# Attention with a score threshold, then a top-1 mixture of experts: tables, gathers, weights, loads and logits around the seam placed elsewhere, and fp16 weights of three double tiles made by VectorE

## The chip, the cores and the metric

One core of a Trainium2 chip runs the whole program in one launch. The metric is the device time of that program in microseconds (us); lower is better. Engines are named as in the profile: PE (TensorE matmuls), PEld (its weight loads), DVE (VectorE), ACT (ScalarE), POOL (GpSimd), SP (SyncE, which here only issues DMAs).

## The reference

Shapes: q, k, v are 8 x 8 x 576 x 64 (batch, heads, tokens, head size), tau is 0.02; w_gate is 512 x 8, w1 is 8 x 512 x 1024, w2 is 8 x 1024 x 512. All are float32.

```python
scores = scale * q @ k^T
thresh = max(scores, axis=-1) - tau
scores = where(scores >= thresh, scores, -1e9)
attn = exp(scores - max); attn = attn / (sum(attn) + 1e-9)
x = (attn @ v), heads side by side        # 4608 tokens x 512
logits = x @ w_gate
expert_idx = argmax(logits); gate_w = its softmax probability
for e in range(8):
    xe = x[expert_idx == e]
    out[expert_idx == e] = gate_w * (max(xe @ w1[e], 0) @ w2[e])
```

## The kernel before, in words

**Attention.** The 64 heads are worked as 32 pairs, the 8 batches as four pairs each. A pair takes 11 steps (st_order, s_order): each step makes one 128 x 512 tile of scores of a later pair (s_unit, whose row minima of the negated scores go to nm, L368) and one transposed tile of this pair (st_unit, st, L404 and L405). fp32 is kept by splitting numbers into fp16 high and low parts, so a product is three fp16 matmuls, or two wider ones through the stacked tiles QK, CQ and ck. On each transposed tile ACT makes the exponential e (L421), DVE sets what is below the threshold to zero (mask, L424), and for each double tile of 1024 columns ACT casts to the fp16 weights ph (L429) and POOL makes the remainder pl (L430), one of them on DVE for the last pair (PLV). av_piece (L474) multiplies ph and pl with the values.

**The row maxima** of a pair are turned by PE (turn in parts, pst, L379), the threshold is added and split in three fp16 rows by a chain over ACT and DVE (L384 to L387), and SP puts these rows into CQ (L392). The next pair's transposed tiles wait for them.

**After each batch** (finish): ACT and DVE make the reciprocals of the sums, one(j) makes a 128-token tile of x (xn, L528), high splits it into the row buffer R (L535 cast, L536 rest), SP turns it with a DMA transpose (xTg, L543), logits multiplies it with the gate (lg, L561), route finds the expert of each token on DVE (L591 to L602), ranks counts the places by matmuls (rk, L610 to L613), and POOL scatters the rows R into the DRAM buffer xs, sorted by expert (L633). For the last batch b = 7 the logits are spread over steps (LS) and route's chain is put into the plan at once.

**The expert part** runs slots of 128 tokens: tables0, tables1 and tables2 (after the routes of batches 5, 6 and 7) compute on DVE which rows of xs a slot reads (counts with pc, L663; table_first, L683 to L692; row, L658). fetch(m) gathers a slot on POOL (Rm, spare or R <- xs, L850) and SP turns it (xTm, L860); gemm1 makes h (L914, relu on ACT L902 and DVE L903), gemm2 makes y (L947), ACT scales it (L958) and POOL scatters it to the output (L961). Slots 0 to 2 use tiles of their own, slots 3 and 4 the tile "spare", later slots the five parts of R, which are free only once the rows of batch 7 were scattered. The order of the halves is written in `turns`: first gemm1 of slots 0, 1, 2, then gemm2 of 0 and 1, gemm1 of 3, gemm2 of 2, and so on.

**Expert weights.** An expert has eight chunks of 128 x 1024 fp32 (w1: four, w2: four): load_w issues the DMA (wf, L794), split_w casts the high half on ACT (wb, L809) and makes the low half on DVE (L817). For expert 0 the low half goes over PE: the high half is multiplied with the identity into PSUM (hi_w, L254), and DVE subtracts it (L255).

**What sets the order.** A plan: plan(k, f) puts work at step k, after(d, f) d steps on. hurry gives work a higher priority. A step is one round of the main loop; in it due() runs the planned work at three places (FRONT, MID, END). The expert part is a generator, experts(), of chunks of about 12 matmuls; RATE(k) says how many chunks are issued in a step: 0 before KM = KEND - km, rate/100 from there to KEND = 352 (the end of the last pair's steps), 1 after. moe(c, ...) puts work at chunk c. Numbers of the plan are in TUNE. The five engines then run their own queues in the order so written (moved a little by the scheduler where program order isn't kept), and wait for each other by semaphores. SP's queue is in order: a DMA whose data isn't there yet holds all DMAs behind it.

The touched places: TUNE, the tiles cks and cqs, parts.turn, st_unit.mask and cast, ranks (its last lines), load_w, tables0 to tables2, and the plan of the split_w and load_w of expert 0. The line numbers here and in the rows are those of the kernel before; in the changed kernel they are 3 lines more at L392, 11 more at L430, L536 and L591, and 18 more from L794 on.

## Time and profile before

| | us |
|---|---|
| median of three runs | 1001.75 (998.88 to 1005.34) |
| the profiled execution, its own time | 997.49 |
| its span in the trace | 995.8 |
| PE busy | 941.6 (95%) |
| DVE busy | 700.4 (70%) |
| ACT busy | 654.1 (66%) |
| POOL busy | 563.1 (57%) |

The mean granted clock of PE over the span was 0.983. All times in the rows below are those of one profiled execution, counted from the start of its span; the 1.7 us between the span and that execution's own time lie around it. The attention's pairs run from about 20 to 575 us, the seam between the two parts lies between about 520 and 660 us, and the expert part fills the rest.

### The profile page before, as it was taken

What the parts mean: (1) busy time and instruction counts of PE and PEld (TensorE: products, weight loads), DVE (VectorE), ACT (ScalarE), POOL (GpSimd) and SP (SyncE); (2) the same over time, 40 slices, a digit from 0 to 9 for tenths busy, and PEclk for the clock granted to TensorE, in tenths of its full rate; (3) what the DMA queues carried; (4) which work ended last, traced back from release to release, by engine and by line L of the source; (5) the groups of instructions that cost most, each with busy time, mean ns of one, the idle gap of its engine ahead of it and who ended that gap; (6) DMA issues with size and microseconds to landing.
All of it is one profiled execution on the core that took longest, in us unless ns stands there. A gap on an engine that the chain in (4) does not pass through costs nothing. (4 is left out here: it accounts for less than half of the span.)

```text
span 995.8 us, 28654 instructions
## 1 busy us (share of the span) xinstructions
PE 941.6 (95%) x11548; PEld 606.9 (61%) x11548; DVE 700.4 (70%) x1413; ACT 654.1 (66%) x1114; POOL 563.1 (57%) x470
## 2 busy tenths in 40 slices
PE   7899999999999999999998998799999999999997
PEld 2355556556566555565664675677666776667684
DVE  7899999989999889999999664816342333423560
ACT  2689897988989888989989853534243332433651
POOL 6366886895986977969969851343122121221121
PEclk8899999999999999999999899999999999999999
DMA  7553454464555646546636569998664756556630
GB/s 199 146 137 75 140 141 134 121 170 113 148 153 137 160 96 175 146 113 161 150 91 193 88 171 276 379 188 247 170 218 116 224 151 180 164 156 214 217 109 27
DMA packets 142750, 159.20 MB, mean 160 GB/s; under 512 B 96403, under 2 KB 112789, under 8 KB 142614
## 3 DMA queue, kind: packets, MB, share of 16 engines
q1 hardware_dynamic: 126598, 100.33, 39.9%
q0 software_dynamic: 9248, 29.45, 9.1%
q10 hardware_dynamic: 6768, 27.55, 8.8%
q8 instruction: 92, 1.51, 0.6%
q14 instruction: 44, 0.36, 0.1%
HBM read 90.24 MB, written 19.44 MB: 110 GB/s over the span
## 5 line engine op out<-in xcount | busy, mean ns | idle before, releaser
L430 POOL TENSOR_TENSOR pl<-e,ph 128x1024 f16<-128x1024 f32 x158 | 335.8, 2133 | 102.3 <-ACT ph L429 64.0
L421 ACT ACTIVATE e<-st,ntau 128x512 f32<-128x512 f32 (+1 forms) x352 | 222.7, 649 | 53.0 <-PE st L405 49.2
L424 DVE SCALAR_TENSOR_TENSOR e<-st,e 128x512 f32<-128x512 f32 (+1 forms) x352 | 220.3, 636 | 11.2 <-ACT e L421 10.5
L947 PE MATMUL y<-wb,hl 128*128 128x512 f16 (+1 forms) x1056 | 202.9, 361 | 0.0
L368 DVE TENSOR_REDUCE nm<-s 128x1 f32<-128x512 f32 x300 | 188.4, 633 | 20.4 <-PE s L358 18.4
L914 PEld LDWEIGHTS <-wb 128*128 128x128 f16 x2304 | 189.4, 98 | 19.8 <-issue 1.5
L914 PE MATMUL h<-xTm,wb 128*128 128x256 f16 (+2 forms) x2112 | 194.7, 253 | 1.0 <-DMA xTm<-Rm 1.0
L474 PE MATMUL av<-vop,ph 128*128 128x65 f16 (+3 forms) x3072 | 187.9, 195 | 2.3 <-ACT x L484 2.0
L474 PEld LDWEIGHTS <-ph 128*128 128x128 f16 (+1 forms) x3072 | 158.8, 100 | 46.4 <-issue 21.7
L474 PE MATMUL av<-vop,pl 128*128 128x65 f16 (+1 forms) x1536 | 167.8, 194 | 5.4 <-POOL pl L430 5.2
L429 ACT CAST ph<-e 128x1024 f16<-128x1024 f32 x160 | 166.3, 1039 | 6.1 <-DVE e L424 5.7
L474 PEld LDWEIGHTS <-pl 128*128 128x128 f16 (+1 forms) x1536 | 137.1, 100 | 37.0 <-issue 11.2
L947 PEld LDWEIGHTS <-hl 128*128 128x128 f16 (+1 forms) x1056 | 94.2, 100 | 98.6 <-issue 3.0
L817 DVE SCALAR_TENSOR_TENSOR wb<-wf,wb 128x1024 f16<-128x1024 f32 x88 | 103.9, 1221 | 56.3 <-ACT wb L809 54.8
L404 PE MATMUL st<-QK 128*128 128x512 f16 (+3 forms) x640 | 139.3, 296 | 1.5 <-DVE lo L255 0.8
L405 PE MATMUL st<-CQ,ck 128*128 128x512 f16 (+3 forms) x640 | 137.8, 290 | 0.5 <-DMA CQ<-ptT 0.5
L356 PE MATMUL s<-QK 128*128 128x512 f16 (+1 forms) x600 | 129.1, 292 | 2.9 <-DMA QK<-hi 2.1
L358 PE MATMUL s<-ck,CQ 128*128 128x512 f16 (+1 forms) x600 | 127.6, 288 | 1.5 <-DMA CQ<-hi 1.5
L961 POOL DMA_INDIRECT out_dram<-o,gt x40 | 47.8, 1194 | 138.6 <-ACT o L958 128.1
L809 ACT ACTIVATE wb<-wf 128x1024 f16<-128x1024 f32 x96 | 98.0, 1050 | 35.5 <-DMA wf<-in_w_dram 18.6
L902 ACT ACTIVATE hl<-h 128x512 f16<-128x512 f32 (+1 forms) x80 | 45.8, 572 | 109.9 <-PE h L914 108.3
L865 DVE COPY gt<-R 128x1 f32<-128x1 f32 x33 | 5.0, 153 | 129.7 <-DMA out_dram<-o,gt 112.5
(195 smaller groups left out, 1018.4 us busy)
## 6 DMA issues: line engine op xcount, KB each, us to landing
wf<-in_w_dram SPq DMA_DIRECT2D x96, 512.0 KB
qkf<-in_qk_dram ACTq DMA_DIRECT2D x30, 576.0 KB
vf<-in_v_dram ACTq DMA_DIRECT2D x15, 640.0 KB
QK<-hi SPq DMA_DIRECT2D x64, 144.0 KB
QK<-lo SPq DMA_DIRECT2D x64, 72.0 KB
QK<-hi SPq DMA_DIRECT2D x64, 72.0 KB
ck<-lo SPq DMA_DIRECT2D x64, 72.0 KB
CQ<-hi SPq DMA_DIRECT2D x64, 64.0 KB
```

The lines of the kernel that those rows point to most:

```text
L356: nc.tensor.matmul(sc[rows, oc], d["QA"][a][:, cols], d["KB"][a][:, CH[c]], start=True, stop=False)
L358: nc.tensor.matmul(sc[rows, oc], d["CQ"][:, at:at + cols.stop - cols.start], d["CK"][a][:, CH[c]], start=False, stop=True,)
L368: nc.vector.tensor_reduce(o, sc[:, 0:width(t)], axis=AX.X, op=ALU.max, negate=True)
L404: nc.tensor.matmul(sc[rows, oc], d["KB"][a][:, cols], d["QA"][a][:, CH[c]], start=True, stop=False)
L405: nc.tensor.matmul(sc[rows, oc], d["CK"][a][:, cols], d["CQ"][:, q], start=False, stop=True)
L421: nc.scalar.activation(pf, sc, AF.Exp, bias=ntau, scale=0.125 / SS)
L424: nc.vector.scalar_tensor_tensor(pf, sc, 0.0, pf, ALU.is_ge, ALU.mult)
L429: nc.scalar.copy(h, pd)
L430: (nc.vector if (n, t) in PLV else nc.gpsimd).tensor_tensor(l, pd, h, ALU.subtract)
L474: nc.tensor.matmul(av[:, 0:D] if z == 2 else av, l if z == 1 else h, vop[:, tv, W:W + D] if z == 2 else vop[:, tv, 0:W], start=i in (0, NT ...
L914: nc.tensor.matmul(o, Wt[:, c, wh, f], x, start=c == 0 and z == 0, stop=c == 3 and z == 2,)
L947: nc.tensor.matmul(o, h[:, hh], Wt[:, f, wh, c], start=f == 0 and z == 0, stop=f == 7 and z == 2)
```

## The change

- **Weights made by DVE.** For the last pair's tiles 2, 3, 8, REST, 6 and 7 (three double tiles) the fp16 weights ph come from a second DVE instruction, h = (sc >= 0) * pf with fp16 output, for each of the six tiles; the ACT cast of these three double tiles is gone. POOL's (or DVE's) remainder pl stays.
- **Expert 0's late chunks.** The tiles ck and CQ are allocated in twos, and the fp32 chunks w2[2] and w2[3] of expert 0 are loaded into the halves that are dead by then, at steps 2 and 3 of pair 30, by SP; before they went through the two wf buffers at KEND + 1 and KEND + 3. The last four splits of expert 0 stand at KEND + 1, 3, 5, 7; before at KEND + 1, 3, 9, 12.
- **Expert 1's loads** are issued by ACT's queue; before by SP's. They are 4 steps apart (w1d; before 5), and their splits are planned from chunk 26 on, 4 apart (w1a, w1b; before chunk 22, 5 apart).
- **Expert part's start.** km 12 (16) and rate 40 (15): four chunks are issued before KEND; before two.
- **Logits and ranks of the last batch.** lg7 is 22 (14): the logits stand 8 steps later. The ranks follow 6 steps after the route's start; before at once.
- **Tables.** tables0 and tables1 run 5 steps after the ranks; before after all scatters of their batch. Their fetches stay at the old place (lag). tables0 is hurried no longer.
- **Threshold of the last two pairs.** The transpose pst takes a bank of the scores' pool; for the last pair its chain is planned at once and hurried.

```diff
-lg7=14, km=16, rate=15, w1d=5, w1a=-42, w1b=5
+lg7=22, km=12, rate=40, w1d=4, w1a=-38, w1b=4
...
-    cks = [[cpool.tile([P, S], F16, name=f"ck_{i}_{a}") for a in range(2)] for i in range(NQ)]
-    cqs = [op.tile([P, 9 * P], F16, tag=f"CQ{i}", name=f"CQ_{i}", bufs=1) for i in range(NQ)]
+    ck2 = [cpool.tile([P, 2, 2, S], F16, name=f"ck_{i}") for i in range(NQ // 2)]
+    cq2 = [op.tile([P, 2, 9 * P], F16, tag=f"CQ{i}", name=f"CQ_{i}", bufs=1) for i in range(NQ // 2)]
+    cks = [[ck2[i // 2][:, i % 2, a] for a in range(2)] for i in range(NQ)]
+    cqs = [cq2[i // 2][:, i % 2] for i in range(NQ)]
...
-            ps = ps_m.tile([P, 512], F32, tag="m", name=f"pst_{n}")
+            pool, tag = (ps_sc, "sc") if n >= NPAIR - 2 else (ps_m, "m")
+            ps = pool.tile([P, 512], F32, tag=tag, name=f"pst_{n}")
...
-            chain(1, [
+            chain(int(n < NPAIR - 1), [
...
-            ])
+            ], n == NPAIR - 1)
...
-        (after if n >= 1 else lambda k, f: hurry(f)())(1, turn)
+        if n == 0:
+            hurry(turn)()
+        else:
+            after(1, hurry(turn) if n == NPAIR - 1 else turn)
...
+        direct = n == NPAIR - 1 and t in DIRECT
+
         def mask():
+            if direct:
+                nc.vector.scalar_tensor_tensor(h[:, j], sc, 0.0, pf, ALU.is_ge, ALU.mult)
...
-            nc.scalar.copy(h, pd)
+            if not direct:
+                nc.scalar.copy(h, pd)
...
-                after(wait + dist * n, TABLES[b])
+                at = 5 if b < B - 1 else wait
+                after(at, lambda: TABLES[b](wait + dist * n - at))
-        after(0 if b == B - 1 else RK[b], ranks)
+        after(6 if b == B - 1 else RK[b], ranks)
...
+        if (e, w) == (0, 1) and c >= 2:
+            wf = (ck2, cq2)[c - 2][0]
...
+            nc.sync.dma_start(wf, w12[e, :, c, w])
+            return
-            load = nc.sync.dma_start(wf, w12[e, :, c, w])
+            load = (nc.scalar if e == 1 else nc.sync).dma_start(wf, w12[e, :, c, w])
...
+    DIRECT = (2, 3, 8, REST, 6, 7)
...
-        t = k + WS0 + WSD * i if i < 4 else KEND + (1, 3, 9, 12)[i - 4]
+        t = k + WS0 + WSD * i if i < 4 else KEND + 1 + 2 * (i - 4)
         plan(t, lambda i=i: split_w(*wseq[i]))
-        if i + 2 < 8:
+        if i < 4:
             plan(t, lambda i=i: load_w(*wseq[i + 2]))
-    TABLES = {B - 3: hurry(tables0), B - 2: tables1, B - 1: tables2}
+        elif i >= 6:
+            plan(NSTEP * (NPAIR - 2) + i - 4, lambda i=i: load_w(*wseq[i]))
+    TABLES = {B - 3: tables0, B - 2: tables1, B - 1: tables2}
```

POOL's queue before, at the end of the attention: R is the low half of a row tile of batch 6, pl a double tile's remainder, Rm the gathers of slots 0 and 1.

```order
L536 TENSOR_TENSOR R<-xn_3_12175,R 128x4x128
L430 TENSOR_TENSOR pl_6_12201<-e_6_12199,ph_6_12200 128x1024
L430 TENSOR_TENSOR pl_0_12318<-e_0_12316,ph_0_12317 128x1024
L850 DMA Rm_12214<-xs,row_12173 128x514
L850 DMA Rm_12258<-xs,row_12173 128x514
L430 TENSOR_TENSOR pl_2_12351<-e_2_12349,ph_2_12350 128x1024
```

The same place of POOL's queue in the changed kernel (its L868 is L850 of before, L441 is L430):

```order
L547 TENSOR_TENSOR R<-xn_3_12167,R 128x4x128
L868 DMA Rm_12202<-xs,row_11771 128x514
L868 DMA Rm_12248<-xs,row_11771 128x514
L441 TENSOR_TENSOR pl_6_12193<-e_6_12191,ph_6_12192 128x1024
L441 TENSOR_TENSOR pl_0_12310<-e_0_12308,ph_0_12309 128x1024
L441 TENSOR_TENSOR pl_2_12350<-e_2_12348,ph_2_12349 128x1024
```

The two gathers moved ahead of two remainders.

SP's queue before, at the last batch: xTg are the transposes of its rows R, spare and xTm those of slots 3 to 6, wf the weight loads from in_w_dram (of expert 1, and from wf_0_0_13782 on some of expert 2).

```order
L860 DMA_TRANSPOSE spare<-spare 128x8x128 x2
L860 DMA_TRANSPOSE xTm_13555<-Rm_13554 128x8x128
L860 DMA_TRANSPOSE xTm_13890<-Rm_13889 128x8x128
L543 DMA_TRANSPOSE xTg_0_13430<-R 128x8x128 x2
L794 DMA wf_1_0_13469<-in_w_dram 128x1024
L543 DMA_TRANSPOSE xTg_2_13473<-R 128x8x128 x2
L543 DMA_TRANSPOSE xTg_4_13506<-R 128x8x128
L794 DMA wf_2_0_13546<-in_w_dram 128x1024
L794 DMA wf_3_0_13572<-in_w_dram 128x1024
L794 DMA wf_0_1_13594<-in_w_dram 128x1024
```

SP's queue there in the changed kernel:

```order
L878 DMA_TRANSPOSE spare<-spare 128x8x128
L554 DMA_TRANSPOSE xTg_0_13447<-R 128x8x128 x2
L878 DMA_TRANSPOSE spare<-spare 128x8x128
L878 DMA_TRANSPOSE xTm_13546<-Rm_13545 128x8x128
L554 DMA_TRANSPOSE xTg_2_13494<-R 128x8x128 x2
L554 DMA_TRANSPOSE xTg_4_13523<-R 128x8x128
L878 DMA_TRANSPOSE xTm_13777<-Rm_13776 128x8x128
L812 DMA wf_0_0_13677<-in_w_dram 128x1024
```

Expert 1's loads left SP's queue (the wf that is left is expert 2's); the first two transposes for the logits now stand behind one slot's transpose instead of four. ACT's queue in the changed kernel issues the loads of expert 1 between its casts of the last batch's rows (L546), relus (L920) and weight casts (L827):

```order
L812 DMA wf_0_0_13396<-in_w_dram 128x1024
L920 ACTIVATE hl_0_13261<-h_1_13264 128x512
L546 CAST R<-xn_0_13413 128x4x128
L546 CAST R<-xn_1_13427 128x4x128
L812 DMA wf_1_0_13466<-in_w_dram 128x1024
L920 ACTIVATE hl_0_13471<-h_0_13400 128x512
L827 ACTIVATE wb_1_13393<-wf_0_0_13396 128x1024
L546 CAST R<-xn_2_13443 128x4x128
L546 CAST R<-xn_3_13464 128x4x128
L920 ACTIVATE hl_0_13471<-h_1_13474 128x512
L827 ACTIVATE wb_1_13393<-wf_1_0_13466 128x1024
L546 CAST R<-xn_4_13490 128x4x128
```

None of these loads was in ACT's queue before. DVE's queue before, over the route of the last batch, from the maxima mx to the new counts run, with the low halves of expert 1's and 2's weights (wb) and of relus (hl) between:

```order
L591 TENSOR_REDUCE mx_13743<-lg_13599 128x5
L592 TENSOR_TENSOR lg_13599<-lg_13599,mx_13743 128x40
L817 SCALAR_TENSOR_TENSOR wb_1_13371<-wf_1_1_13644,wb_1_13371 128x2x512
...
L598 TENSOR_REDUCE lg_13599<-oh_13745 128x8
L602 TENSOR_TENSOR run<-run,lg_13599 128x8
```

The same stretch in the changed kernel, whole:

```order
L602 TENSOR_REDUCE mx_13823<-lg_13695 128x5
L603 TENSOR_TENSOR lg_13695<-lg_13695,mx_13823 128x40
L835 SCALAR_TENSOR_TENSOR wb_1_13394<-wf_3_1_13675,wb_1_13394 128x2x512
L604 TENSOR_TENSOR ex_13826<-lg_13695,mx_13823 128x40
L605 TENSOR_TENSOR lg_13695<-lg_13695,rank_108 128x40
L606 TENSOR_REDUCE mw_13824<-lg_13695 128x5
L607 TENSOR_TENSOR oh_13825<-lg_13695,mw_13824 128x40
L835 SCALAR_TENSOR_TENSOR wb_0_11660<-wf_1_0_13800,wb_0_11660 128x1024
L609 TENSOR_REDUCE lg_13695<-oh_13825 128x8
L613 TENSOR_TENSOR run<-run,lg_13695 128x8
```

Two low halves of weights stand inside the chain; before there were five of them and two of relus (hl).

## Rows read from the trace of the kernel before

**Rows 1.** The page, part 1: busy time, share of the span, instructions.
```profile
PE 941.6 (95%) x11548; PEld 606.9 (61%) x11548; DVE 700.4 (70%) x1413; ACT 654.1 (66%) x1114; POOL 563.1 (57%) x470
```

**Rows 2.** Windows: length, busy PE, PEld, DVE, ACT, POOL; PEclk, DMA share, GB/s.
```profile
525.00:550.00 25.00, 19.49 (x258) 10.87 (x257) 21.43 (x50) 23.51 (x43) 24.38 (x19) 0.98 0.65 168
550.00:575.00 25.00, 23.70 (x467) 18.64 (x467) 17.29 (x37) 20.99 (x39) 21.99 (x18) 0.88 0.48 100
575.00:600.00 25.00, 23.15 (x373) 18.70 (x373) 18.39 (x43) 13.17 (x27) 11.72 (x11) 1.00 0.70 162
600.00:625.00 25.00, 20.03 (x232) 13.08 (x230) 11.01 (x17) 10.89 (x15) 2.80 (x3) 0.93 1.01 309
625.00:650.00 25.00, 22.29 (x250) 16.64 (x251) 21.53 (x72) 11.92 (x19) 11.15 (x10) 0.93 0.94 351
650.00:675.00 25.00, 25.00 (x271) 18.83 (x269) 5.08 (x13) 8.14 (x11) 10.43 (x14) 1.00 0.92 175
```

**Rows 3.** Windows of the three stretches at half clock in the seam.
```profile
549.00:556.00 7.00, 6.63 (x99) 4.47 (x99) 4.50 (x15) 4.03 (x10) 6.52 (x5) 0.51 0.68 110
603.60:607.10 3.50, 3.02 (x23) 1.36 (x24) 0.00 (x0) 0.00 (x0) 0.00 (x0) 0.51 1.01 233
627.50:631.00 3.50, 3.29 (x47) 3.30 (x48) 1.70 (x4) 1.61 (x4) 0.67 (x1) 0.51 1.02 408
```

**Rows 4.** Timeline of PE: start, us, line, tiles, idle before and releaser.
```profile
560.75 0.83 PE L914 MATMUL h<-xTm,wb 128*128 128x128 f16 x12 [1.03 <-DMA xTm<-Rm]
...
588.35 0.59 PE L254 MATMUL hi_w<-wb,ident_h 128*128 128x512 f16 x2 [1.79 <-ACT wb L809]
...
604.09 0.48 PE L561 MATMUL lg<-wg,xTg 128*128 128x8 f16 x12 [2.66 <-DMA xTg<-R]
...
627.71 0.19 PE L610 MATMUL rk<-oh,before 128*128 128x8 f16 x1 [5.02 <-DVE run L602]
...
660.15 0.44 PE L914 MATMUL h<-xTm,wb 128*128 128x128 f16 x5
```

**Rows 5.** Timeline of POOL, the gathers of slots 0, 1 and 7.
```profile
548.63 4.20 POOL L430 TENSOR_TENSOR pl<-e,ph 128x1024 f16<-128x1024 f32 x2
553.00 1.01 POOL L850 DMA_INDIRECT Rm<-xs,row  x1 [0.16 <-issue]
...
646.14 0.99 POOL L850 DMA_INDIRECT R<-xs,row  x1 [4.97 <-DVE at_e L745]
```

**Rows 6.** Timeline of SP's queue: start, time held, DMA.
```profile
556.43 10.74 SPq L860 DMA_TRANSPOSE xTm<-Rm  x3
...
595.19 5.50 SPq L860 DMA_TRANSPOSE xTm<-Rm  x2
600.79 2.66 SPq L543 DMA_TRANSPOSE xTg<-R  x2
603.54 0.54 SPq L794 DMA_DIRECT2D wf<-in_w_dram  x1
...
608.99 32.90 SPq L794 DMA_DIRECT2D wf<-in_w_dram  x22
```

**Rows 7.** The page, part 5: the groups of pl, of the mask and of the cast.
```profile
L430 POOL TENSOR_TENSOR pl<-e,ph 128x1024 f16<-128x1024 f32 x158 | 335.8, 2133 | 102.3 <-ACT ph L429 64.0
...
L424 DVE SCALAR_TENSOR_TENSOR e<-st,e 128x512 f32<-128x512 f32 (+1 forms) x352 | 220.3, 636 | 11.2 <-ACT e L421 10.5
...
L429 ACT CAST ph<-e 128x1024 f16<-128x1024 f32 x160 | 166.3, 1039 | 6.1 <-DVE e L424 5.7
```

**Rows 8.** Timeline of ACT, the cast of expert 1's second weight chunk.
```profile
607.71 1.06 ACT L809 ACTIVATE wb<-wf 128x1024 f16<-128x1024 f32 x1 [7.51 <-DMA wf<-in_w_dram]
```

**Rows 9.** Timeline of DVE, first, a middle and last row of the route.
```profile
619.11 0.20 DVE L591 TENSOR_REDUCE mx<-lg 128x5 f32<-128x40 f32 x1
...
624.85 1.22 DVE L817 SCALAR_TENSOR_TENSOR wb<-wf,wb 128x1024 f16<-128x1024 f32 x1
...
627.49 0.16 DVE L602 TENSOR_TENSOR run<-run,lg 128x8 f16<-128x8 f16 x1
```

More of the change, by code (lines that the diff above doesn't have):

```diff
@@ L45 @@
 TUNE = dict(
-    lead=10, cast=2, sl=8, ll=15, sp0=3, sps=0, lv=-16, sv0=-6, sv1=2, av=2, g=4, l=3, d=4, g5=4, l5=3, d5=2, g6=1, l6=2, d6=2, g7=1, l7=1, d7=1, off=2, off5=1, off6=5, lg=4, lg7=14, km=16, rate=15, dh=1, do=3, ws0=6, wsd=2, w1d=5, plv=1, xv=5, so=0, sto=0, ord=0, sc=6, fa=3, fd=4, wa1=-70, wa2=-86, wl1=-28, wl2=-6, avb=1, route=1, ranks=7, pp=8, ew=4, maskat=0, w1a=-42, w1b=5,
+    lead=10, cast=2, sl=8, ll=15, sp0=3, sps=0, lv=-16, sv0=-6, sv1=2, av=2, g=4, l=3, d=4, g5=4, l5=3, d5=2, g6=1, l6=2, d6=2, g7=1, l7=1, d7=1, off=2, off5=1, off6=5, lg=4, lg7=22, km=12, rate=40, dh=1, do=3, ws0=6, wsd=2, w1d=4, plv=1, xv=5, so=0, sto=0, ord=0, sc=6, fa=3, fd=4, wa1=-70, wa2=-86, wl1=-28, wl2=-6, avb=1, route=1, ranks=7, pp=8, ew=4, maskat=0, w1a=-38, w1b=4,
 )
@@ L791, in load_w @@
         i = int(e != 0)
+        if (e, w) == (0, 1) and c >= 2:
+            wf = (ck2, cq2)[c - 2][0]
+            wf = wf.rearrange("p a b s -> p (a b s)") if c == 2 else wf.rearrange("p a s -> p (a s)")
+            wq[e, w, c] = wf = wf.bitcast(F32)[:, 0:F]
+            nc.sync.dma_start(wf, w12[e, :, c, w])
+            return
         wq[e, w, c] = wf = pools[i].tile([P, F], F32, tag="wf", name=f"wf_{e}_{c}_{w}", bufs=2 + 6 * i)
         if e in range(E):
-            load = nc.sync.dma_start(wf, w12[e, :, c, w])
+            load = (nc.scalar if e == 1 else nc.sync).dma_start(wf, w12[e, :, c, w])
             if e == 1:
@@ L1046, in level, with tables0, tables1, tables2 @@
         return cnt, s_e
-    def tables0():
+    def tables0(lag):
         T[0] = level("0", ((), EARLY[0]), None)
         for m in range(NF):
-            after(1 + m, lambda m=m: fetch(m))
-    def tables1():
+            after(lag + 1 + m, lambda m=m: fetch(m))
+    def tables1(lag):
         T[1] = level("1", EARLY, T[0])
         for m in range(2):
-            after(1 + m, lambda m=m: fetch(NF + m))
-    def tables2():
+            after(lag + 1 + m, lambda m=m: fetch(NF + m))
+    def tables2(lag):
         cnt, s_e = level("2", (EARLY[1], None), T[1])
```

## The prediction

> **What bounds the kernel now.** I read the page's busy times first: PE works 941.6 of the 995.8 us of the span, 95%, and no other engine over 70% [rows 1]. So PE bounds the kernel as a whole, and a change that keeps PE's instructions can gain only what PE idles, or works at a lower clock. The windows come second, since a mean says nothing of a place: at the seam PE is busy 19.49, 23.70, 23.15, 20.03 and 22.29 of five stretches of 25 us, and from 650 us on all of it [rows 2]. The idle time between 525 and 650 us is thus 5.5 + 1.3 + 1.9 + 5.0 + 2.7 = 16.3 us. Third, the clock. In the same windows it falls to 0.88 and 0.93, and narrow windows show why: it is at 0.51, the half level (1.2 instead of 2.4 GHz), in three stretches of 7.0, 3.5 and 3.5 us, in which PE has work nearly all the time [rows 3]. Half of 14 us, 7.0 us, is lost there. Together 23.3 us is the most that can be had in this stretch. Each half-clock stretch stands within a few us of a wait of PE, so I count it with that wait.
>
> Fourth, the timeline of PE says who ends the waits [rows 4]: 1.03 us for slot 0's transpose xTm, 1.79 us for a weight cast of ACT before hi_w, 2.66 us for the first xTg before lg, and 5.02 us for run, the end of the route, before rk. The last slot of the seam, h of slot 7 at 660.15, has no wait.
>
> Fifth, the engine that ends a wait is followed back. For xTm: POOL makes two remainders pl from 548.63, 4.20 us, and only then gathers slot 0 at 553.00 [rows 5]; SP turns it from 556.43 and PE starts at 560.75, 4.3 us on [rows 4, 6]. For xTg: SP is held by two transposes of slots for 5.50 us, and issues xTg at 600.79 [rows 6]. For run: the second weight load of expert 1 goes out at 603.54, and the rest from 608.99 on behind the xTg, in 32.90 us for 22 loads [rows 6]. ACT idles 7.51 us for the load issued at 603.54 and casts it at 607.71 [rows 8], so a load takes 4.2 us from issue to cast. All these casts and their low halves fall together with the route: from mx at 619.11 to run at 627.49 DVE takes 8.4 us [rows 9], in which the listing has five low halves of weights (1.22 us each) and two of relus.
>
> **The change, part by part.**
>
> *Gathers of slots 0 and 1.* They stand two pl earlier on POOL: 4.2 us [rows 5]. If PE is there by then, h starts at 556.5 instead of 560.75. PE's own wait is only 1.03 us; to be there earlier it must also lose what the half-clock stretch from 549 to 556 costs, half of 7.0, 3.5 us [rows 3, 4]. So this part is worth 1.0 us if the half clock stays, and 4.2 us at most. That stretch comes after 25 us in which PE idled 5.5 us, in small waits [rows 2]; the tables now start 5 steps after the ranks, earlier, and some of these waits should go with them. I take 1.0 plus half of the 3.5, 2.7 us. What is late next: the two pl that were passed come up to 2.0 us later (two gathers of 1.0), and av waits for pl. POOL is 24.38 of 25 us busy there [rows 2], so there is no slack to make it up; this is the first rival.
>
> *Weights by DVE.* Six mask-like instructions at 0.64 us, 3.8 us more on DVE; three casts at 1.04 us, 3.1 us less on ACT [rows 7]. DVE has 25 - 17.29 = 7.7 us idle between 550 and 575, ACT only 4.0 [rows 2]. The pl after them then wait for DVE, not for a cast that comes two steps later. I count it at nothing; without that cover it would cost up to the 3.8 us, if it helps the pl it gains at most one cast, 1.0 us.
>
> *Expert 0's late chunks.* Loaded at pair 30, they are there when ACT wants them; before, they were issued after the attention's end, behind SP's slot transposes (10.74 us from 556.43) [rows 6]. The 1.79 us before hi_w [rows 4] can go, but ACT's cast (1.06 us) [rows 8] must still come before it. Between 0 and 1.8 us; I take 1.5, near the upper end, since the splits are also closer together and the data is no longer waited for.
>
> *Logits.* With the spare gathers' table earlier, and one slot's transpose ahead of xTg instead of four, xTg goes out earlier on SP; the logits also stand 8 steps later behind PE work of y and h. Both ends of the 2.66 us move apart, so I count the wait as gone, and the half-clock stretch right behind it (603.6 to 607.1, 3.5 us, half lost) with it: 2.7 + 1.7 = 4.4 us; the other end is 0.
>
> *Expert 1's loads and the ranks.* Eight loads leave SP's queue, where the second was issued at 603.54 although the windows show the DMA engines only 0.70 busy between 575 and 600 [rows 2, 6]. On ACT's queue they stand among the casts of x rows. The low halves come before the route instead of inside it: two are left between mx and run, so at least 8.4 - 3 x 1.22 = 4.7 us are left by the rows, and less where both relus are gone too. The ranks are 6 steps later. I count the 5.02 us and the half-clock stretch of 627.5 to 631 (half of 3.5) as gone, 6.7 us, less a rest of 0.6 us: 6.1 us. Its bounds are 0 (the chain stays as long as it was) and 6.7.
>
> One rule bears on this part. The queue was the limit here by the rows: SP stood, with the DMA engines not full. The Trainium skill (DMA: Bandwidth & Descriptors, "Issuing engines are not separate DMA queues") says against such a move that DMAs of all engines share the same 16 DMA engines, and that issuing from several only saves the sequencer's time. By that rule alone the loads would come no sooner; the trace disagrees in so far as SP's time was waiting for other DMAs' data, not issue.
>
> *What may become late.* The gathers into R for slots 5 and later must wait until the last batch's rows were scattered, and the ranks are put later. Slot 7's gather was at 646.14. For slot 0 it was 3.4 us from gather to transpose and 4.3 from there to h [rows 4 to 6], so slot 7 was there at about 653.9, and h wants it at 660.15: 6 us of room. With PE some 14 us ahead and the gathers one output scatter later in POOL's order the room is about nothing; the wait that this brings is 0 to 3 us, I take 0.5.
>
> *Rest.* The order of attention's first 29 pairs is the same on all engines; I count nothing, and 1 us either way.
>
> The sum: 2.7 + 1.5 + 4.4 + 6.1 - 0.5 = 14.2 us of the 23.3. The profiled execution falls from 997.49 to 983.3. The median of the runs was 4.26 us above that execution, so the median is forecast at 987.5.
>
> **The rivals.**
>
> *First: the end of attention gives back what it gains.* POOL is full from 525 to 565, DVE is 21.43 of 25 us busy from 525 to 550 [rows 2]. Tables put earlier add small DVE instructions just there, and pl is 2.0 us later. Then the first two parts (2.7 + 1.5) bring nothing, the others 4.4 + 6.1 - 0.5 = 10.0: 991.7. For it: no busy engine there loses work before 550. Against it: the three casts and expert 0's late loads leave ACT and SP near the end.
>
> *Second: the change doesn't do what it says at the ranks.* The weight halves only move; loads that come no sooner, or a DVE that is busy with expert 2's halves, leave run as late as before, and rk waits on. Then 6.1 us is missing: 14.2 - 6.1 = 8.1, 993.6. For it: the DMA engines are at 1.01 and 0.94 between 600 and 650 [rows 2], so that loads may be the limit. Against it: 0.70 before 600.
>
> *Third, on the other side: ACT's queue is held by the loads.* A load that must wait for its memory (the last pair's tiles, whose room wf takes) stops everything behind it on ACT: relus, casts of x rows, and with them xTg, lg and the route. Its price: at 4.2 us for each of eight loads, 33.4 us [rows 6, 8], against 25 - 10.89 = 14.1 us that ACT idles in the window from 600 to 625 [rows 2]; 19.3 us come out late, and the logits' and ranks' gains are lost: 997.49 - 2.7 - 1.5 + 19.3 + 4.26 = 1016.8. It decides once the holds add up to more than the 14.1 us (1.8 us a load). At SP's own rate for such loads, 32.90 / 22 = 1.5 us, they add up to 12 and cost nothing. For it: nothing shields ACT, and the list of its queue has two loads ahead of row casts. Against it: by then the tiles that they replace are dead for some us.
>
> **How the numbers follow.** The forecast has 0.56, the first rival 0.18, the second 0.18, the third 0.08. Runs of this kernel lie 0.6% apart, so about 1% (10 us) can be told from no change. The forecast and half of the first rival lie below 991.7, and a small part of the second: 0.56 + 0.09 + 0.03 = 0.68 faster. The other halves, 0.09 + 0.15 = 0.24, are within 1%; 0.08 is slower. The range: at the low end nearly all of 23.3 us is had, 997.49 - 23.3 + 4.26 = 978.5, so 978; at the high end both other rivals lie inside, with a rest wait of 3 us at slot 7 and 4 us of run to run difference above the second: 1000.
>
> **What would show it.** In the trace of the changed kernel: PE's first h starts 4 us sooner against the end of POOL's pl than it did; no wait over 1 us before hi_w and lg; the route from mx to run takes 4.7 us or less instead of 8.4, and rk waits under 1 us; PE idle between 525 and 650 falls from 16.3 us to about 7, and at most one half-clock stretch is left there. Wrong would be: a wait of ACT over 4 us at a weight load with relus behind it (third rival), rk waiting 4 us or more for run (second), or new waits for pl between 540 and 560 with a half-clock stretch as long as before (first).

## The result, and the profile after

The changed kernel is slower. Its median is 1012.53 us (six runs, 1010.26 to 1018.67) against 1002.43 us for the kernel before (six runs as well): ratio 1.0103, 95% interval 1.0063 to 1.0142. The forecast was 987.5 us, and its range ended at 1000. The profiled execution of the changed kernel took 1012.50 us with a span of 1010.7, so between the two profiled executions lie 14.9 us of span.

First the page of the changed kernel: busy times and share of the span as in [rows 1], then two groups (busy us, mean ns | idle time before them and what ended most of it). The last line is the second group in the kernel before.

```profile
PE 946.6 (94%) x11548; PEld 609.3 (60%) x11548; DVE 704.5 (70%) x1419; ACT 650.7 (64%) x1111; POOL 557.3 (55%) x470
...
L440 ACT CAST ph<-e 128x1024 f16<-128x1024 f32 x157 | 163.2, 1039 | 7.5 <-DVE e L434 7.2
...
L932 PE MATMUL h<-xTm,wb 128*128 128x256 f16 (+2 forms) x2112 | 201.1, 256 | 8.5 <-issue 8.3
```

```profile
L914 PE MATMUL h<-xTm,wb 128*128 128x256 f16 (+2 forms) x2112 | 194.7, 253 | 1.0 <-DMA xTm<-Rm 1.0
```

The count of PE's instructions is as before, so the loss is idle time or clock: over the whole span PE is busy 5.0 us more for the same instructions, and idle 9.9 us more. Three casts less, as meant. New are 8.3 us of idle time before h that no releaser explains ("issue": the profile shows nothing that PE waited for). The windows of [rows 2], now of the changed kernel (us, busy time of PE, PEld, DVE, ACT and POOL, PEclk, DMA share, GB/s):

```profile
525.00:550.00 25.00, 21.83 (x305) 12.48 (x304) 21.78 (x50) 23.79 (x43) 23.95 (x19) 1.00 0.74 203
550.00:575.00 25.00, 21.57 (x415) 17.44 (x412) 20.54 (x43) 20.01 (x41) 19.49 (x16) 0.93 0.40 96
575.00:600.00 25.00, 23.21 (x374) 19.37 (x372) 20.43 (x43) 11.31 (x22) 11.26 (x11) 0.93 0.64 127
600.00:625.00 25.00, 22.39 (x277) 15.67 (x275) 7.29 (x8) 7.41 (x9) 2.98 (x3) 1.00 1.15 251
625.00:650.00 25.00, 15.55 (x157) 10.97 (x158) 14.50 (x30) 12.74 (x19) 8.28 (x7) 0.73 0.90 336
650.00:675.00 25.00, 20.84 (x176) 12.57 (x176) 11.63 (x57) 3.33 (x6) 8.57 (x12) 0.93 0.78 163
```

PE's idle time over the six windows is 150 - 125.4 = 24.6 us; by [rows 2] it was 150 - 133.7 = 16.3. Up to 625 us the changed kernel is ahead by 89.0 - 86.4 = 2.6 us of PE's busy time. Then it loses 6.7 and 4.2 us in two windows. The clock goes with it. Windows of three of its four half-clock stretches in the seam (the fourth is at 570.6, 3.4 us), same columns:

```profile
591.10:594.50 3.40, 3.22 (x31) 3.24 (x32) 2.13 (x6) 2.17 (x4) 0.22 (x1) 0.51 1.09 229
625.20:638.90 13.70, 5.99 (x55) 4.51 (x56) 8.88 (x19) 7.02 (x10) 0.99 (x1) 0.50 1.01 399
666.10:669.50 3.40, 3.03 (x9) 1.26 (x10) 0.89 (x3) 0.60 (x1) 1.15 (x2) 0.51 1.11 183
```

Together 23.9 us at 1.2 GHz, against 14 us in [rows 3]; half of the difference, 5 us, is lost by it. The idle time of the six windows (8.3 more) and the clock (5) make 13.3 of the 14.9 us. The long stretch begins 7.7 us before the wait of rk ends and lasts 6 us beyond it. The timeline of PE (start, us, line, tiles, idle before and releaser) shows the places of [rows 4]:

```profile
613.46 0.46 PE L572 MATMUL lg<-wg,xTg 128*128 128x8 f16 x12 [0.42 <-DMA xTg<-R]
...
632.91 0.19 PE L621 MATMUL rk<-oh,before 128*128 128x8 f16 x1 [10.10 <-DVE run L613]
...
663.40 0.27 PE L932 MATMUL h<-xTm,wb 128*128 128x128 f16 x2 [1.07 <-issue]
664.86 0.33 PE L932 MATMUL h<-xTm,wb 128*128 128x128 f16 x3 [1.18 <-issue]
```

The wait before lg fell from 2.66 to 0.42 us. The wait for run doubled, from 5.02 to 10.10. Why is run late? DVE's timeline ahead of it:

```profile
621.25 1.23 DVE L835 SCALAR_TENSOR_TENSOR wb<-wf,wb 128x1024 f16<-128x1024 f32 x1 [2.08 <-ACT wb L827]
...
627.86 1.23 DVE L835 SCALAR_TENSOR_TENSOR wb<-wf,wb 128x1024 f16<-128x1024 f32 x1 [5.39 <-ACT wb L827]
629.01 0.19 DVE L602 TENSOR_REDUCE mx<-lg 128x5 f32<-128x40 f32 x1
...
632.69 0.16 DVE L613 TENSOR_TENSOR run<-run,lg 128x8 f16<-128x8 f16 x1
```

The logits had ended at 617.1, but mx starts at 629.01. In between DVE stands 5.39 us before a low half of a weight chunk (it is expert 2's first) whose cast ACT has not made. In DVE's list mx stands behind that low half, and it starts as that one ends. Of the low halves of experts 1 and 2, five started ahead of mx in the kernel before and five inside the chain; here eight start ahead of it and two inside. ACT's timeline, where "q" marks a DMA that it issues:

```profile
598.07 2.97 ACTq L812 DMA_DIRECT2D wf<-in_w_dram  x3
...
611.51 1.06 ACT L827 ACTIVATE wb<-wf 128x1024 f16<-128x1024 f32 x1 [6.75 <-DMA xTm<-Rm]
...
620.16 1.06 ACT L827 ACTIVATE wb<-wf 128x1024 f16<-128x1024 f32 x1 [2.73 <-DMA wf<-in_w_dram]
...
626.77 2.95 ACT L827 ACTIVATE wb<-wf 128x1024 f16<-128x1024 f32 x3 [5.56 <-DMA wf<-in_w_dram]
```

ACT idles 6.75 us behind a load that waits for a transpose xTm of SP (in the compiled order both signal their end on the same semaphore, and the load is the later user), and then 2.73 and 5.56 us for weights still on their way. SP's queue (start, time held, DMA) over the same time:

```profile
590.96 8.45 SPq L554 DMA_TRANSPOSE xTg<-R  x2
...
600.86 4.08 SPq L878 DMA_TRANSPOSE xTm<-Rm  x1
605.03 7.96 SPq L554 DMA_TRANSPOSE xTg<-R  x3
...
614.45 31.89 SPq L812 DMA_DIRECT2D wf<-in_w_dram  x16
```

Each xTg holds SP for 2.0 to 4.5 us, although the rows R that it turns were ready; by [rows 6] two took 2.66 us together. Expert 2's first load leaves at 614.45, and ACT casts it at 626.77, 12.3 us later. The 4.2 us of [rows 6, 8] are no measure for it: in the kernel before the same load left at 613.7 and was cast 9.7 us later, but mx did not stand behind it.

```profile
623.36 1.04 ACT L809 ACTIVATE wb<-wf 128x1024 f16<-128x1024 f32 x1
```

### The profile page after: what moved, and what is told of

Its sections match the earlier page's. It is cut to its first block, busy times and chain, and to the rows that moved or that the text cites. A ratio compares the mean times of both kernels' runs of the same rounds, so it can differ in the third digit from the quotient of the medians.

```text
span 1010.7 us, 28648 instructions
## 1 busy us (share of the span) xinstructions
PE 946.6 (94%) x11548; PEld 609.3 (60%) x11548; DVE 704.5 (70%) x1419; ACT 650.7 (64%) x1111; POOL 557.3 (55%) x470
## 5 line engine op out<-in xcount | busy, mean ns | idle before, releaser
L441 POOL TENSOR_TENSOR pl<-e,ph 128x1024 f16<-128x1024 f32 x158 | 335.6, 2133 | 104.3 <-ACT ph L440 66.8
L434 DVE SCALAR_TENSOR_TENSOR e<-st,e 128x512 f32<-128x512 f32 (+1 forms) x352 | 219.9, 636 | 10.2 <-ACT e L427 9.0
L932 PEld LDWEIGHTS <-wb 128*128 128x128 f16 x2304 | 193.1, 100 | 30.6 <-issue 12.0
L932 PE MATMUL h<-xTm,wb 128*128 128x256 f16 (+2 forms) x2112 | 201.1, 256 | 8.5 <-issue 8.3
L370 DVE TENSOR_REDUCE nm<-s 128x1 f32<-128x512 f32 x300 | 188.0, 632 | 16.3 <-PE s L360 14.3
L440 ACT CAST ph<-e 128x1024 f16<-128x1024 f32 x157 | 163.2, 1039 | 7.5 <-DVE e L434 7.2
L979 POOL DMA_INDIRECT out_dram<-o,gt x40 | 44.0, 1099 | 161.4 <-ACT o L976 143.0
L920 ACT ACTIVATE hl<-h 128x512 f16<-128x512 f32 (+1 forms) x80 | 45.8, 572 | 120.9 <-PE h L932 102.6
L827 ACT ACTIVATE wb<-wf 128x1024 f16<-128x1024 f32 x94 | 95.6, 1049 | 36.8 <-DMA wf<-in_w_dram 15.0
L976 ACT ACTIVATE o<-y,gt 128x512 f32<-128x512 f32 (+1 forms) x40 | 26.6, 664 | 99.8 <-PE y L965 82.0
```

Of the source, the lines that this page charges most:

```text
L370: nc.vector.tensor_reduce(o, sc[:, 0:width(t)], axis=AX.X, op=ALU.max, negate=True)
L434: nc.vector.scalar_tensor_tensor(pf, sc, 0.0, pf, ALU.is_ge, ALU.mult)
L440: nc.scalar.copy(h, pd)
L441: (nc.vector if (n, t) in PLV else nc.gpsimd).tensor_tensor(l, pd, h, ALU.subtract)
L932: nc.tensor.matmul(o, Wt[:, c, wh, f], x, start=c == 0 and z == 0, stop=c == 3 and z == 2,)
```

## The experiments

Two theories: Q, expert 1's loads on ACT's queue run beside SP's transposes and make both late; O, what stands ahead of mx in DVE's list makes run late, whatever the queue. Ratios are against the kernel before on the same chip, with 95% intervals. The runs were made on three chips, on which the kernel before took 1000.74, 995.06 and 996.46 us, so times of different chips are compared by their ratios only.

**Loads back on SP (e1_loads_on_sp).** The changed kernel with

```diff
-        load = (nc.scalar if e == 1 else nc.sync).dma_start(wf, w12[e, :, c, w])
+        load = nc.sync.dma_start(wf, w12[e, :, c, w])
```

> The changed kernel with the eight loads of expert 1 issued by SP again, all else kept. Theory Q (the queue: on ACT's queue the loads run beside SP's transposes, whose issue takes 2.0 to 4.5 us each instead of 1.25, and one load holds ACT 6.75 us): the transposes take about 1.3 us again, the first lg starts some 5 us sooner, the wait of rk for run falls from 10.1 to 5 us or less, and the time to about 1000 to 1004. Theory O (the order on DVE: mx stands behind a low half whose data comes late, whoever issues the load): the loads go out behind the transposes, the low halves ahead of mx come as late as now, rk still waits 8 us or more, and the time stays at 1009 to 1014. Theory S (logits and ranks 8 and 6 steps later are the loss by themselves): no difference, 1012.

Measured: 1000.63 us, 0.9993 [0.9965, 1.0020]. The whole loss is gone with this one line, and theory S with it, as the later logits and ranks were kept. But it did not go in the way that theory Q had it: the transposes xTg still hold SP for 1.26 to 3.29 us (median 2.26), so ACT's loads are not all that slows them, and the first lg starts later, not sooner (612.83, in the changed kernel 609.62). What comes sooner is mx, at 624.84 instead of 629.01: from 618 us on DVE waits 0.21 us at most before it. PE still waits for run:

```profile
628.09 0.19 PE L621 MATMUL rk<-oh,before 128*128 128x8 f16 x1 [4.00 <-DVE run L613]
```

**The route kept ahead (route_kept_ahead).** The changed kernel with the order on DVE pinned: the low halves of experts 1 and 2, mx and run stay in the order in which the program writes them, which puts three low halves behind run that stood ahead of it.

```diff
+        if e in (1, 2):
+            tc.keep_in_program_order(low)
...
+            lambda: (tc.keep_in_program_order if b == B - 1 else id)(
+                nc.vector.tensor_reduce(mx, Lj, axis=AX.X, op=ALU.max)),
...
+            lambda: (tc.keep_in_program_order if b == B - 1 else id)(tt(run, run, got, ALU.add)),
```

> The changed kernel with DVE's order fixed so that the low halves of expert 1's last chunk and of expert 2's first two stand behind the route of the last batch, not ahead of or inside it; all loads stay where they are. Theory O: mx starts at about 622.5 instead of 629.0 and run is done 1.7 us later, rk's wait falls from 10.1 to about 1.5 us, the half-clock stretch of 13.7 us behind it goes with it or shrinks to 3.4, and the time falls by 9 to 15 us, to 998 to 1004. Theory Q: the late casts and loads hold the chain whatever stands where; rk's wait falls by less than 3 us, and the time to no less than 1008. Theory S: the same, 1010 or more.

Measured: 1000.91 us, 1.0009 [0.9980, 1.0039]. This also takes the loss away. mx to run is now 1.68 us (627.82 to 629.50), and rk does not wait. But PE comes to rk no sooner than in the changed kernel (632.91), with 42 matmuls of h less done: the wait moved to the last lg. The loads on ACT's queue still run beside the transposes, and SP's queue shows it:

```profile
627.30 0.48 PE L572 MATMUL lg<-wg,xTg 128*128 128x8 f16 x12 [8.47 <-DMA xTg<-R]
...
633.37 0.17 PE L622 MATMUL rk<-oh,before 128*128 128x8 f16 x1
```

```profile
602.88 8.48 SPq L554 DMA_TRANSPOSE xTg<-R  x2
611.46 3.57 SPq L881 DMA_TRANSPOSE xTm<-Rm  x2
615.12 1.57 SPq L554 DMA_TRANSPOSE xTg<-R  x1
```

So the time is the one that theory O named, but not by its way, in which mx was to start at 622.5. In this profile PE is busy 943.7 us instead of 946.6, and the idle time before h without a releaser is 2.2 us instead of 8.3 (us, times, the longest):

```profile
PE h L935 <- issue: 2.2, 6, 0.5
```

**The same order in the kernel before (before_route_kept_ahead)**, same edit on the kernel before.

> The kernel before with the same fix of DVE's order: five low halves of weights and one of relus stand no longer between mx and run. Theory O: mx stays at about 619, run is done at 621 instead of 627.5, PE comes to rk at 622.7 and waits 0 instead of 5.0 us, the half-clock stretch of 3.4 us goes: 5 to 7 us less than before, 995 to 997. Theory Q (the data is late, not the order): rk waits 3 us or more still, within 2 us of before.

Measured: 995.54 us, 0.9950 [0.9922, 0.9978], in the range expected. PE's timeline: rk waits no more, and two waits are left, that of pc a new one. The half-clock stretch that was to go is still there (627.4, 3.4 us), now behind pc.

```profile
611.78 0.46 PE L561 MATMUL lg<-wg,xTg 128*128 128x8 f16 x12 [2.80 <-DMA xTg<-R]
...
626.96 0.17 PE L664 MATMUL pc<-run,ones 128*128 128x8 f16 x1 [3.38 <-DVE posi L620]
```

**Only the loads moved, in the kernel before (before_e1_loads_on_act)**: the line of the first experiment, put into the kernel before.

> The kernel before with only the eight loads of expert 1 moved to ACT's queue. Theory Q: the transposes of the last batch take 2 to 4 us each instead of 1.25, lg comes 3 to 8 us later, ACT is held once for several us by a load that waits for a transpose, and the time rises by 3 to 10 us, to 1005 to 1012. Theory O: the loads come sooner and only two low halves are left in the route, so rk waits less and the time falls by 2 to 6 us, to 996 to 1000.

Measured: 1008.46 us, 1.0082 [1.0045, 1.0118]. The move alone makes a loss of nearly the size of the whole change's. PE's timeline has the last of three waits for xTg, 1.04, 2.30 and

```profile
621.09 0.48 PE L561 MATMUL lg<-wg,xTg 128*128 128x8 f16 x12 [6.54 <-DMA xTg<-R]
```

rk does not wait here; the loss lies before it, at lg (15.1 us of waits in the whole trace, before 3.1). It is one issue, the last of five, that takes 5.24 us; theory Q had expected 2 to 4 us of each. But the issue is not all of a transpose: the one issued at 610.27 had PE waiting until 621.09, 10.8 us, and in the kernel before the one issued at 600.79 until 604.09, 3.3 us [rows 4, 6]. The view of the tile xTg gives for SP's issues the least, the median and the longest in ns, first of this kernel, then of the kernel before:

```profile
L543 SPq DMA_TRANSPOSE xTg<-R x5: 1259/1326/5239, 598.4 to 611.7; - x5
```

```profile
L543 SPq DMA_TRANSPOSE xTg<-R x5: 1231/1282/2093, 600.8 to 607.7; - x5
```

**Both repairs (sp_loads_and_route_ahead)**: the edits of the first two experiments in the changed kernel.

> The changed kernel with both repairs: expert 1's loads on SP's queue, and the low halves of weights behind the route on DVE. Theory QO (both together make the loss at the ranks, each takes most of it away): the 4.0 us that rk still waits with the loads on SP go, and with them the half-clock stretch of 6.8 us at 626: 5 to 7 us less than with the loads on SP alone, 993 to 996. Rival (one repair is enough, what is left lies elsewhere): the time stays at 999 to 1001 and another wait takes rk's place.

Measured: 992.72 us, 0.9964 [0.9938, 0.9990]. By the ratios this is 0.3%, 3 us, less than with the loads on SP alone, not 5 to 7, and it does not come from rk, as theory QO had it: rk waits 5.55 us, there 4.00, and the half-clock stretch is 6.8 us in both. What is absent here is the idle time before h without a releaser, 5.6 us there. PE's wait, then DVE's timeline, which says why:

```profile
623.27 0.19 PE L622 MATMUL rk<-oh,before 128*128 128x8 f16 x1 [5.55 <-DVE run L614]
```

```profile
620.23 1.23 DVE L836 SCALAR_TENSOR_TENSOR wb<-wf,wb 128x1024 f16<-128x1024 f32 x1 [0.67 <-ACT wb L828]
621.37 0.19 DVE L603 TENSOR_REDUCE mx<-lg 128x5 f32<-128x40 f32 x1
...
623.05 0.16 DVE L614 TENSOR_TENSOR run<-run,lg 128x8 f16<-128x8 f16 x1
```

A low half of expert 1 itself is ahead of mx in the program's order, and the pin keeps it there.

**Without DVE's weights (repaired_without_direct)**: the kernel of the last experiment with

```diff
-    DIRECT = (2, 3, 8, REST, 6, 7)
+    DIRECT = ()
```

> The changed kernel with both repairs and the list DIRECT empty: ACT casts the last pair's three double tiles again, DVE has six instructions less. Theory D (in the changed kernel PE waits 2.4 us at 569.9 for the mask e of DVE, since DVE has 3.8 us more to do before it): that wait and the half-clock stretch of 3.4 us behind it go, 2.5 to 4.5 us less than with both repairs alone, 990 to 992. Rival (DVE's six instructions lie beside other work): within 1.5 us of it; or 1 to 3 us slower, if the casts of ACT hold up pl.

Measured: 991.55 us, 0.9965 [0.9942, 0.9989], against 0.9964 with them. The three double tiles on DVE cost or bring nothing that these runs can tell (each interval reaches some 2.5 us to either side). The wait of st for DVE's e, first in the changed kernel and then here, stayed, so they are not its cause:

```profile
569.91 0.38 PE L410 MATMUL st<-QK 128*128 128x512 f16 x1 [2.37 <-DVE e L434]
```

```profile
568.20 0.59 PE L410 MATMUL st<-QK 128*128 128x512 f16 x1 [3.34 <-DVE e L434]
```

**Expert 0's late chunks (before_route_ahead_late_chunks)**: before_route_kept_ahead with the changed kernel's home and time for expert 0's last two chunks.

```diff
+        if (e, w) == (0, 1) and c >= 2:
+            wf = (ck2, cq2)[c - 2][0]
...
+            nc.sync.dma_start(wf, w12[e, :, c, w])
+            return
```

> The kernel before with the route kept ahead on DVE, and with the part of the change that loads expert 0's last two chunks into the dead ck and CQ tiles and splits them at KEND + 5 and 7. By the prediction: the waits of hi_w (0.4 and 0.6 us in the trace with the route ahead) go, and SP, with no load ahead of it, turns the rows for the logits sooner, so that the 2.8 us of lg go too: 2 to 4 us less than 995.5. Rival: the splits now crowd ACT and DVE where they are busy, 0 to 2 us more.

Measured: 996.84 us, 0.9997 [0.9974, 1.0020], against 0.9950 without it. The waits before hi_w for these chunks (0.6 us at most) are gone, but h waits 0.91 us, lg 1.02 and 3.36 instead of 2.80, and pc 3.79 instead of 3.38; the slots' transposes start 8 us later.

**DVE's weights in the kernel before (before_route_ahead_direct)**: before_route_kept_ahead with DIRECT as in the changed kernel.

> The kernel before with the route kept ahead on DVE, and with the weights of the three double tiles made by DVE (DIRECT) as the only part of the change. Theory D: PE waits for DVE's mask in the last pair, 2 to 4 us more than 995.5, 997 to 1000. Rival (hidden, as the prediction has it): within 1.5 us of 995.5.

Measured: 994.05 us, 0.9980 [0.9953, 1.0007]. The interval overlaps that without them, so a gain or loss of some 2 us can't be told. The wait that theory D named is not in the trace: st waits 0.2 us for DVE's e.

**Loads on ACT's queue, but later (act_loads_after_the_casts).** The changed kernel, with the loads still on ACT:

```diff
-                after(W1D * i, lambda x=x: load_w(*x))
+                after(10 + 3 * i, lambda x=x: load_w(*x))
```

> The changed kernel with expert 1's loads still on ACT's queue, but planned 10 steps later and 3 steps apart, so that at most the last row's cast stands behind one. Theory Q1 (the harm is that weight loads are in flight while SP turns the last batch's rows): SP's transposes xTg take 1.3 to 2 us each instead of 2.0 to 4.5, the last lg ends 3 us or more sooner than at 617, and the time falls by 3 to 8 us against the changed kernel (a ratio to before of 1.002 to 1.007), less than by the repairs, since the low halves stand inside the route. Theory Q2 (the harm is ACT's queue itself, held at each load that shares a completion semaphore with a transpose): ACT is held for 4 us or more again, and the ratio stays at 1.008 to 1.012.

Measured: 995.59 us, 0.9989 [0.9961, 1.0018], better than either theory expected. So the queue by itself is not the harm; the moment matters. Two loads leave among the five transposes, and the median issue of xTg is 1.45 us instead of 3.68. But the last lg ends only 1.4 us sooner (615.7), not 3, and run is done at 633.2, no sooner than in the changed kernel (632.9). rk waits less because PE has more work ahead of it, 480 matmuls of h and 81 of y instead of 451 and 72, and h waits for late weights in its place. The trace also has no idle time before h without a releaser, which is a part of what it gains on the changed kernel. That the harm is loads beside transposes is thus argued here, not shown. The tile view, then PE's timeline:

```profile
L554 SPq DMA_TRANSPOSE xTg<-R x5: 1261/1453/4383, 595.5 to 605.0; - x5
```

```profile
621.02 0.39 PE L932 MATMUL h<-spare,wb 128*128 128x128 f16 x2 [2.85 <-ACT wb L827]
...
633.29 0.18 PE L621 MATMUL rk<-oh,before 128*128 128x8 f16 x1 [1.60 <-DVE run L613]
```

**Expert 1's second matrices later.** Three kernels with their splits 14 chunks later (in the last two the rank sums are pinned too): repaired_w2_behind_route on both repairs, before_w2_behind_route on the kernel before with the route ahead, before_direct_w2_behind_route the same with DIRECT.

```diff
-            k = 64 + TUNE["w1a"] + TUNE["w1b"] * i
+            k = 64 + TUNE["w1a"] + TUNE["w1b"] * i + 14 * w
```

> The changed kernel with both repairs, and with the w2 chunks of expert 1 split 14 chunks later, so that one instead of three of their low halves stands ahead of mx on DVE. With both repairs alone rk still waited 5.55 us. Theory O: mx comes 2 to 4 us sooner, rk's wait falls to 0 to 2.5 us and the half-clock stretch behind it from 6.8 to 3.4 us or none: 3 to 6 us less than with both repairs, a ratio to before of 0.990 to 0.994. Rival (the one that is left, wf_1_2_1, comes as late as all three, since its load is behind the others): no difference, 0.996.

> The kernel before with the route and the sums of the ranks kept ahead of the low halves and the w2 chunks of expert 1 split 14 chunks later, without DIRECT. Theory O: 0.988 to 0.992 of before, 3 to 7 us better than the route kept ahead alone is not expected, since rk waited 0 there already: 1 to 3 us from pc (3.4 us of wait). Rival (waits of lg for the transposes are the bound now): 0.994 to 0.996.

> The kernel before with the route and the sums of the ranks kept ahead of the low halves, the w2 chunks of expert 1 split 14 chunks later, and the weights by DVE (DIRECT). Theory O: no low half of w2 stands before mx, rk waits 0, and pc, which waited 2.5 us for the ranks' sums, waits under 1 us: 0.988 to 0.992. Theory D (DIRECT costs 2 to 4 us in the kernel before): it is 0.2 to 0.4% slower than the next kernel, which differs from it by DIRECT alone. Rival: the same within 0.15%.

Measured: 0.9990 [0.9966, 1.0014], 1.0009 [0.9979, 1.0039], 0.9990 [0.9960, 1.0020]. All miss. In the first, rk waits 5.54 us as before it: another low half, at 620.68, still stands ahead of mx at 621.82, which is the reason that the rival gave. In the second pc waits 0.97 us instead of 3.38, as meant, but y waits 2.2 us for DVE's hl. The last two differ by DIRECT alone, and their intervals overlap.

**The stalls before h: three more profiles.** The changed kernel twice more and e1_loads_on_sp once more, as they are.

> The changed kernel as it is, profiled once more. Still open is a part of the loss that no experiment named: in the changed kernel's profile PE idles 8.3 us before matmuls of h with no releaser (17 waits in rows 0.74 us apart; the 96 matmuls of one slot took 10.9 us instead of 5.5), in the kernel before none. Theory S (these stalls belong to the changed kernel): they stand in this execution too, 5 to 11 us of idle at the same slots (588 to 591, 646 to 650 and 660 to 667 us), with a time of 1010 to 1018. Theory E (they belong to single executions, whatever the kernel): under 2 us of them here, or at other slots, and a time that is not above the other runs for lack of them, or 4 to 8 us below 1012.5. In both, rk waits 8 to 11 us for run and the half-clock stretch behind it is 10 to 14 us long, as those come from the order and the loads.

> Expert 1's loads on SP's queue, profiled once more (its first profile had 5.6 us of such stalls of h, in an execution of 1005.1 us, the slowest of its ten, whose median was 1000.6). Theory S: 4 to 7 us of stalls again at the same two slots, at about 1000 to 1005. Theory E: under 2 us here, or at other slots, at 996 to 1001. rk waits 3 to 5 us in both.

> The changed kernel a third time, so that theory E does not rest on one execution. Theory S: 5 to 11 us of stalls of h at the same slots, 1010 to 1018. Theory E: another amount or another place than in the first two profiles, with a time that moves with it by the stalls' length.

Measured, one execution each: 1010.78, 1001.30 and 1012.70 us (kernel before 1004.37). PE's waits for h in the three (us, times, the longest of one place):

```profile
PE h L932 <- issue: 6.3, 13, 1.1
```

```profile
PE h L932 <- issue: 6.7, 15, 1.2
```

```profile
PE h L932 <- issue: 7.6, 15, 1.1
```

They come back at the same slots, the third, sixth, seventh and eighth that PE begins (with the loads on SP the third and seventh at first, now all four): theory S. They belong to the program, and to both of these kernels, so they are not made by ACT's loads alone; the kernel with the loads on SP has them and is no slower than the kernel before. rk waits 9.3 and 9.9 us in the two profiles of the changed kernel, and 1.7 in the other, less than the 3 to 5 that both theories expected; the half-clock stretch at rk is 10.2 us in both. ACT's hold behind a transpose is 3.43 us in the third profile and absent in the second, where ACT stands 8.96 us for a weight load instead: the hold by the semaphore is one form, late loads are the common cause.

## Why the prediction was wrong

**Where it went.** The two repairs form a square in the changed kernel: neither 1.0103, SP's loads 0.9993, the pinned route 1.0009, both 0.9964. Either takes away about 1%, both 1.4%. In the changed kernel's trace late loads make the cast late, the cast holds a low half, the low half holds mx, and rk waits. With the loads on SP this wait falls from 10.1 to 4.0 us (1.7 in the second profile). With the order pinned it only moves to lg, and with both it is 5.55 us. So the two repairs do not share one wait, and what the pin gains in the changed kernel is not explained; in the profiles it goes with the idle time before h without a releaser (8.3, then 2.2 us; 5.6, then none).

Shown: that the loads do harm on ACT's queue at that moment, by e1_loads_on_sp (all of the loss) and before_e1_loads_on_act (+0.8% alone); that the queue alone does not, by act_loads_after_the_casts; and that DVE's order costs 0.5% in the kernel before, by before_route_kept_ahead. Not separated: how much of the first is slower transposes, how much ACT's own standing behind its loads, and how much the idle time before h, as every run here changed more than one of them.

**Expert 1's loads and the ranks, counted at 6.1 us: the step that failed.** It took run to be late by what stands between mx and run, and there it was right: that part of the route fell from 8.4 to 3.7 us (629.01 to 632.69), below its 4.7. It didn't ask what stands ahead of mx. The low halves that it took out of the chain went ahead of mx instead, and mx waited there for the last of their loads. Instead of a gain of 6.1 us the wait grew by 5.1 and its half-clock stretch from 3.5 to 13.7 us: 5.1 + 10.2 / 2 = 10.2 us lost.

**The rule that it set aside.** SP was waiting and the windows showed the DMA engines 0.70 busy, so the step took the queue for the limit. That was misread twice. The load at 603.54 lies in the next window, whose share is 1.01 [rows 2]. And 0.70 is a mean over 25 us; narrower windows, two of the kernel before and one of the changed kernel, columns as in [rows 2], show little room or none where the loads were to go:

```profile
590.00:600.00 10.00, 10.00 (x106) 6.79 (x103) 9.03 (x17) 3.81 (x7) 4.75 (x6) 1.00 0.98 182
600.00:604.00 4.00, 1.43 (x7) 0.46 (x5) 0.69 (x1) 0.20 (x1) 0.00 (x0) 0.96 0.84 160
```

```profile
591.00:599.40 8.40, 8.12 (x73) 6.26 (x74) 7.13 (x13) 4.80 (x7) 0.78 (x2) 0.80 1.20 151
```

In the changed kernel five of the loads go out between 586 and 601 us, and the transposes beside them take a median of 3.68 instead of 1.28 us. The Trainium skill (DMA: Bandwidth & Descriptors, "Issuing engines are not separate DMA queues") says that DMAs issued from several engines still run on the same DMA engines. The trace agrees for the loads that count: the second to sixth of expert 1's chunks were cast 2 to 11 us sooner than in the kernel before, but the eighth some 6 us later and expert 2's first 3.4 us later, and mx stood behind that one.

**Logits, 4.4 us.** The wait did go (2.66 to 0.42 us), and the half-clock stretch at 603.6 with it, but because PE came later: the last lg ended at 617.1 us, before at 612.5. A wait that shrinks is no gain when the work behind it ends later.

**Gathers of slots 0 and 1, 2.7 us.** h came 4.3 us sooner (556.47 instead of 560.75), as marked, but was given back: PE is 2.3 us busier in 525 to 550 and 2.1 us less in 550 to 575, where st waits 2.37 us for DVE's e and 0.94 for CQ. That is the first rival for this part; DVE is busy 20.54 us there, before 17.29. What makes e late was not isolated: not DIRECT, and not the late chunks, as the wait stands in every profile of the changed kernel and its variants and none built on the kernel before has one over 0.3 us.

**Expert 0's late chunks, 1.5 us.** The wait before hi_w went; alone, the part did not gain (0.9997 against 0.9950 without it, with intervals that only touch).

**Weights by DVE, nothing.** Right as far as these runs can tell: 0.9965 without, 0.9964 with.

**What may become late, 0.5 us.** No slot waited for its gather. The 6 to 8 us of stalls before h, idle time without a releaser, were not foreseen and are in no term of the sum; they are the other large piece of the idle time.

**The rivals.** The third had the right place (ACT's queue, relus and route behind it) and the wrong price: it put the point at holds of 14.1 us in sum, while ACT's one hold was 6.75 us and two of three profiles have one; that its 1016.8 us lie near the measured time is luck. The second was right that the weight halves only move and rk waits on, and wrong in the time, as it left the other gains standing. Both were given too little, as the step asked only whether loads leave sooner, not whether the last of them lands sooner. Of the signs that were named, h 4 us sooner, a route of 4.7 us or less and no wait over 1 us before lg came; against them rk waited 10.10 us, PE idled 20.4 us from 525 to 650 and not 7, and three half-clock stretches stand there instead of one.

**The best version.** before_route_kept_ahead (0.9950), sp_loads_and_route_ahead (0.9964) and repaired_without_direct (0.9965) beat both kernels; these runs don't tell them apart.

## What to carry to other kernels

Before a load is moved to another engine's queue, list what transposes and gathers fly at that moment: an idle queue is not idle DMA engines, and a mean over 25 us hides a full stretch of 10. Ask what stands ahead of the critical instruction on its engine's list, as well as what stands inside its chain. Where an order matters, pin it; in the kernel before that alone gained 0.5%, without moving a byte. And when a repair brings the time that was expected, look whether the wait went or only moved.

## What the runs showed of the hardware that was not expected

PE stalls before matmuls of h without a releaser, in rows of waits some 0.74 us apart with one to five matmuls between. The 96 matmuls of one slot take 10.9 us in the changed kernel; in the kernel before they take 5.5. In sp_loads_and_route_ahead, act_loads_after_the_casts and the kernel before the waits view has none of them, in before_route_kept_ahead 0.3 us, in before_e1_loads_on_act 1.7, in route_kept_ahead 2.2. The clock falls to its half level as the first and the third row end (591.1 and 666.1 us). What makes them in some of these programs, and at the same slots each time, stays open; nothing here was tried against them. One thing was not looked into: instructions come by DMA too (queue q8 in the DMA view, in the kernel before two pieces between 655 and 670 us, in the changed kernel none), and whether PE waited for its own there is not known.

The DMA transposes of the last batch's rows held SP's queue 1.28 us in the median in the kernel before, 3.68 in the changed kernel, and up to 5.24 in before_e1_loads_on_act, with weight loads on ACT's queue beside them. And a load can wait for a transpose of another engine that it shares no data with, through the semaphore that both use (6.75 us on ACT).
